# Starting TensorE's streamed operands 64 bytes into their buffers

## The chip, the cores and the metric

The kernel runs on one core of a Trainium2 chip. The metric is device time in microseconds (us) for one execution. Three executions of the kernel before took 458.63, 458.64 and 460.37 us; their median is 458.64 us.

A core has a matrix engine (TensorE, PE in the profile), which multiplies a *stationary* operand that it has loaded ("holds") by a *moving* operand that it streams past it, both read from the on-chip memory SBUF. The load of the stationary operand is an instruction of its own, shown in the profile as the row PEld. VectorE (DVE), ScalarE (ACT) and GpSimd (POOL) do the elementwise work, and DMA queues move data.

## The reference, cut to what matters

The input x has 2048 tokens of 448 channels. Two blocks follow one another, each behind a layer norm whose scale and shift come from a conditioning vector:

```
h = layernorm(x) * (1 + ca) + sa
q, k, v = split(h @ wqkv)                       # 16 heads of 28 channels
pq, pk = phi(q), phi(k)                         # phi(t) = (t > 0 ? t + 1 : exp(t)) + 1e-6
kv = sum over tokens of pk^T v ; z = sum over tokens of pk
x = x + ga * ((pq @ kv) / (pq . z + 1e-6)) @ wo
h = layernorm(x) * (1 + cb) + sb
u = gelu(h^T @ w1 + b1)                         # contraction over the 2048 tokens, 1792 outputs
x = x + gb * (u @ w2 + b2)^T                    # back to the 2048 tokens
```

The data are float32 and the result has to hold that accuracy. The kernel therefore cuts most operands into a high part, rounded to the fast matmul format (float32r), and a low part, the remainder, and forms high*high + high*low + low*high: three fast matmuls for one product.

## The kernel before, in words

**Tiles.** The 2048 tokens are 16 tiles (`t`) of 128 partitions by 448 channels. Nearly every buffer is a slot of one of two pools: `slot` (76 buffers) and, in the first half, `tslot` (25 buffers). Each slot is padded to 512 floats, which is 2048 bytes in every partition, whatever its use. In the allocation of the built program both pools begin 128 bytes past a multiple of 512; an unused constant tile of 96 floats (`space`, line 85) lies ahead of the second pool. A 128-column slice of a slot begins at a multiple of 512 bytes inside it. So a streamed operand, which is a whole slot from its start, and the slice that TensorE holds for it, begin at the same byte address modulo 256 (and modulo 512).

**Stages and their matmuls.** Each matmul listed here streams 448 columns of float32r past 128 held columns, and each needs a load of its own.

- k and q (`project`, line 312): the transposed, normalized tokens (`hh`, `hl`) are held; the weights (`Whi`, `Wlo`, tiles `wh`, `wl`) are streamed. There are 11 matmuls for each of k and q and each token tile but the first, whose products go through plain float32 (`project0`).
- the sums over tokens (`a_outer`, line 394): the tokens (`xh`, `xl`) are held, phi(k) (`pkh`, `pkl`) is streamed; 11 matmuls for each of 16 tiles, accumulated in four PSUM banks `cacc`.
- the output projection (`b_out`, line 654): the transposed scaled phi(q) (`pth`, `ptl`) is held, the folded matrix (`Wph`, `Wpl`) is streamed; 12 matmuls for each of 16 tiles.
- the first product over tokens (`step`, `acc3`, lines 705 to 707): blocks of w1 (`ph`, `pl`) are held, the normalized tokens (`H2h`, `H2l`) are streamed; 3 matmuls for each of 14 output blocks and 16 token tiles.
- the second product over tokens runs in two forms: `mult7` (lines 889 and 890, tiles `ut` and `uw` streamed, one matmul of 448 and one of 224 columns in turn) and `mult1` (again `acc3`, tile `uw` streamed as two runs of 224 columns; the moving operand of line 706 there begins 896 bytes further on than that of 705).

**Order.** The instruction order is written out by hand in one program (`manual_schedule`); engines meet through semaphores only. TensorE's queue therefore has one order through the whole kernel, and the loops over `t` interleave k, the sums, part of q, the projection and the first product so that the other engines' splitting, norms and copies are done ahead of use.

**Who writes the streamed operands.** High parts: ScalarE copies (`w_high` line 176, `a_pk_parts` line 372, `split` line 70, `b_norm2` line 699). Low parts: VectorE subtractions (lines 71, 182, 351, 702), or, for eleven tiles of phi(k) and two of the weights, a ScalarE copy with the sign turned followed by an accumulating DMA from POOL's queue (lines 194 to 195 and 353 to 354).

Of the kernel before, what the change touches and what calls it, by code (L numbers as in the profile page):

```python
# [9 lines left out]
F32R = mybir.dt.float32r  # L10
# [4 lines left out]
P = 128  # L15
S, D, F = 2048, 448, 1792
NT = S // P
NF = F // P
G = 112
# [23 lines left out]
def block_kernel(ctx: ExitStack, tc: tile.TileContext, x, wqkv, wo, w1, b1, w2, b2, c, wmod, out):  # L43
# [16 lines left out]
    def slot(name, w=D, dt=F32, parts=P):  # L60
        return slots.tile([parts, w], dt, name=name, tag="slot", padded_shape=[P, 512])

    def tslot(name, dt=F32, parts=P, w=D):
        return tok.tile([parts, w], dt, name=name, tag="tok", padded_shape=[P, 512])

    def bank(name):
        return psum.tile([P, 512], F32, name=name, tag="bank")

    def split(full, hi, lo):
        nc.scalar.activation(hi, full, AF.Copy)  # L70
        nc.vector.tensor_sub(lo, full, hi.bitcast(F32))  # L71
# [100 lines left out]
    Whi, Wlo = {}, {}  # L172

    def w_high(j, ch):
        Whi[j, ch] = tslot(f"wh{j}_{ch}", F32R)
        nc.scalar.activation(Whi[j, ch], raw_w[j, ch], AF.Copy)

    def w_low(j, ch):
        w, r = Whi[j, ch], raw_w[j, ch]
        if ch < 3:  # L180
            Wlo[j, ch] = tslot(f"wl{j}_{ch}", F32R)
            nc.vector.tensor_sub(Wlo[j, ch], r, w.bitcast(F32))
        else:
            nc.vector.tensor_sub(w[64:128], r[64:128], w[64:128].bitcast(F32))

    def w_low_dma(j, ch):
        w, r = Whi[j, ch], raw_w[j, ch]
        if ch < 3:
            Wlo[j, ch] = tslot(f"wl{j}_{ch}", F32R)
            lo, hi = Wlo[j, ch], w  # L190
        else:
            lo = hi = w[64:128]
            r = r[64:128]
        nc.scalar.activation(lo, hi.bitcast(F32), AF.Copy, scale=-1.0)
        nc.gpsimd.dma_start(lo, r, accum_op=ALU.add)
# [4 lines left out]
    raws, parts = {}, {}  # L200
# [148 lines left out]
    def low(t, lo, full, hi):  # L349
        if t in DVE_LOW:  # L350
            nc.vector.tensor_sub(lo, full, hi.bitcast(F32))
        else:
            nc.scalar.activation(lo, hi.bitcast(F32), AF.Copy, scale=-1.0)
            nc.gpsimd.dma_start(lo, full, accum_op=ALU.add)
# [13 lines left out]

    def a_pk_parts(t):
        pk = pkf.pop(t)  # L370
        hi, lo = slot(f"pkh{t}", dt=F32R), slot(f"pkl{t}", dt=F32R)
        nc.scalar.activation(hi, pk, AF.Copy)
        low(t, lo, pk, hi)
        if t in (0, 1, NT - 1):
            pksum.append(pk)
        elif t == NT - 2:
            pksum14.append(pk)
        else:
            nc.gpsimd.dma_start(pksum[t % 2], pk, accum_op=ALU.add)
        pks[t] = (hi, lo)  # L380
# [62 lines left out]
    a_first((2, 3))  # L443
    keep_warm(2)
    w_high(1, 0)
    a_copy((0, 1))
    a_copy((2,))
    a_copy((3,))
    del tps[0]
    st.pop(0)  # L450
    a_norm_a(1)
    w_high(1, 1)
    a_norm_b(1, sap[:, :D])
    a_dup(1)
    w_low(1, 0)
    w_high(1, 2)
    w_low(1, 1)
    kp0 = project0(1, "kp", lambda: a_transpose(1))
    a_split(1)
    w_high(1, 3)  # L460
    w_low(1, 2)
    w_low(1, 3)
    mod_out(0, sap)
# [3 lines left out]
    for ch in range(4):  # L467
        w_high(0, ch)
    a_exp(0, kp0)
    w_low_dma(0, 0)  # L470
    a_norm_b(2)
    w_low_dma(0, 1)
    a_stats(3)
    a_dup(2)
# [20 lines left out]
    a_exp(2, kp2)  # L495
    a_norm_b(4)
    a_pk_parts(0)
    a_dup(4)
    a_pk(2, kp2)
    a_phi_q()  # L500
    a_pk_parts(1)
    a_q(2)
    a_high(2)
# [6 lines left out]
    for t in range(3, NT):  # L510
# [15 lines left out]
        a_pk(t, kp)  # L526
        a_phi_q()
        a_pk_parts(t - 1)
        if t + 3 < NT:
            a_stats(t + 3)  # L530
# [14 lines left out]
        if t == 4:  # L545
            for g in range(4):
                w = tslot(f"wo{g}", parts=G)
# [58 lines left out]
    H2h, H2l = [None] * NT, [None] * NT  # L606
# [85 lines left out]
    def b_norm2(t, i):  # L692
        rs = rss[i - 1][:, 1:2]
        nb = small.tile([P, 1], F32, name=f"nb{t}", tag="nb")
        nc.gpsimd.tensor_mul(nb, nm2s.pop(t), rs)
        nc.scalar.activation(ys[t], ys[t], AF.Identity, bias=nb, scale=rs)
        H2h[t] = slot(f"h2h{t}", dt=F32R)
        H2l[t] = slot(f"h2l{t}", dt=F32R)
        nc.scalar.activation(H2h[t], ys[t], AF.Copy)

    def b_low2(t):
# [15 lines left out]
    for g in range(4):  # L717
        wp = bank(f"wp{g}")
        nc.tensor.matmul(wp[:G, :D], kvm[:, g * G:(g + 1) * G], wo_sb[g], start=True, stop=True)
        hi = tslot(f"wph{g}", F32R, G)  # L720
        lo = tslot(f"wpl{g}", F32R, G)
        split(wp[:G, :D], hi, lo)
        Wph.append(hi)
        Wpl.append(lo)
# [3 lines left out]
    for i in range(NT + LAG):  # L728
# [11 lines left out]
        t = i - LAG  # L740
# [19 lines left out]
        if norm2:  # L760
            b_norm2(i - 4, i)
# [229 lines left out]
    for o0, n in W1G[1:]:  # L991
# [5 lines left out]
        for r in range(first, NT):  # L997
# [4 lines left out]
            if xleft and k % 2:  # L1002
                t = xleft.pop(0)
# [13 lines left out]
    for n, (kind, p) in enumerate(order):  # L1017
        if jobs:
            jobs.pop(0)()
        while xleft:  # L1020
            t = xleft.pop(0)
# [40 lines left out]
```

## Time and profile before

| what | value |
|---|---|
| median of 3 executions | 458.64 us |
| the profiled execution, its own time | 458.67 us |
| its span in the trace | 457.0 us |
| TensorE matmul busy | 451.6 us, 99% |
| weight loads busy | 409.9 us, 90% |
| VectorE / ScalarE / GpSimd busy | 356.7 / 241.4 / 90.9 us |
| granted TensorE clock | 1.00 |

The busy time of a matmul row counts from its start to a modelled end, and neighbouring matmuls overlap in it: a matmul shown as 365 ns long can be followed by the next one after 203 ns. What a matmul costs in a packed stream is therefore the distance from its start to the next start, here called the *spacing*; it is read from a timeline of starts, or from a stretch that holds nothing else, divided by the count.

### The profile page before, as it was taken

Reading aid. Unit: us, or ns where it says so; the run is one execution under the profiler, and the core shown is the slowest. Engines: PE = TensorE matmul, PEld = TensorE weight load, DVE = VectorE, ACT = ScalarE, POOL = GpSimd, SP = SyncE. Lnnn points to the kernel's source line nnn. Section 1 sums busy time; section 2 is a strip of 40 time slices with the busy share of each in tenths; the row PEclk is TensorE's granted clock in tenths of the full one; section 3 lists DMA queues with packets and bytes.
Section 4 is the critical chain, followed back from the end, with each engine's and each line's share of the span. In section 5 each row is a group of like instructions: output and inputs, shape, how many; then the busy total and the mean of one; then the engine's idle time right before and its main releaser. Section 6 shows DMA issues by size and latency. Waiting matters only on the chain.

```text
span 457.0 us, 7265 instructions
## 1 busy us (share of the span) xinstructions
PE 451.6 (99%) x2378; PEld 409.9 (90%) x2378; DVE 356.7 (78%) x781; ACT 241.4 (53%) x538; POOL 90.9 (20%) x163
## 2 busy tenths in 40 slices
PE   8999999999999999999999999999999999999996
PEld 7689998998799999988999999999999999999996
DVE  5798897878898898896559676629696977798982
ACT  1648766635456576676665445226556262536350
POOL 2215675620014355554300000000000000000000
PEclk9999999999999999999999999999999999999999
DMA  8969999993200003222407453317960583628312
GB/s 228 287 174 174 172 193 227 210 226 116 70 1 2 23 24 103 61 47 48 126 17 230 162 193 106 112 39 227 288 187 23 177 239 113 176 99 250 112 55 98
DMA packets 60550, 61.85 MB, mean 135 GB/s; under 512 B 9248, under 2 KB 53856, under 8 KB 60512
## 3 DMA queue, kind: packets, MB, share of 16 engines
q1 hardware_dynamic: 54752, 52.45, 38.2%
q0 software_dynamic: 5760, 8.95, 12.0%
q8 instruction: 18, 0.29, 0.3%
q14 instruction: 20, 0.16, 0.1%
HBM read 45.09 MB, written 7.34 MB: 115 GB/s over the span
## 4 chain that ended last, share of the span: by engine, by line
PE 90%; ACT 3%; POOL 2%; DVE 1%; DMA 1%; issue 1%; SPq 1%; DVEq 0%
PE y L889 11%; PE up L705 9%; PE up L707 9%; PE up L706 9%; PE cacc L394 8%; PE kp L312 7%; PE qp L312 7%; PE y L890 5%; PE op L654 5%; PE yp L705 4%; PE yp L707 4%; PE yp L706 4%; PE tp L291 1%; DMA wm<-in_w_mod_dram 1%; PE tq L638 1%; PE modp L169 1%
## 5 line engine op out<-in xcount | busy, mean ns | idle before, releaser
L705 PE MATMUL up<-h2h,ph 128*128 128x448 f32 x224 | 82.2, 367 | 0.0
L706 PE MATMUL up<-h2l,ph 128*128 128x448 f32 x224 | 81.8, 365 | 0.0
L707 PE MATMUL up<-h2h,pl 128*128 128x448 f32 x224 | 81.8, 365 | 0.0
L71 DVE TENSOR_TENSOR pl<-pr,ph 128x512 fp32r<-128x512 f32 (+1 forms) x60 | 36.3, 615 | 13.0 <-ACT ph L70 8.3
L706 PEld LDWEIGHTS up<-h2l,ph 128*128 128x128 f32 x224 | 42.1, 188 | 3.5 <-issue 0.2
L705 PEld LDWEIGHTS up<-h2h,ph 128*128 128x128 f32 x224 | 42.1, 188 | 3.5 <-issue 0.2
L707 PEld LDWEIGHTS up<-h2h,pl 128*128 128x128 f32 x224 | 42.1, 188 | 3.4
L70 ACT ACTIVATE ph<-pr 128x512 fp32r<-128x512 f32 (+1 forms) x60 | 32.8, 567 | 16.3 <-PE up L706 11.4
L895 ACT ACTIVATE cc<-y 128x448 f32<-128x448 f32 x15 | 8.2, 545 | 56.5 <-PE y L890 39.8
L705 PE MATMUL yp<-uw,qw 128*128 128x448 f32 x84 | 31.1, 370 | 0.0
L707 PE MATMUL yp<-uw,qw 128*128 128x448 f32 x84 | 30.7, 366 | 0.0
L706 PE MATMUL yp<-uw,qw 128*128 128x448 f32 x84 | 30.7, 365 | 0.0
L394 PE MATMUL cacc<-pkh,xh 128*128 128x448 f32 x64 | 24.8, 387 | 0.0
L654 PE MATMUL op<-wph,pth 112*128 112x448 f32 x64 | 24.7, 386 | 0.0
L654 PE MATMUL op<-wpl,pth 112*128 112x448 f32 x64 | 23.4, 366 | 0.0
L394 PE MATMUL cacc<-pkl,xh 128*128 128x448 f32 x64 | 23.4, 366 | 0.0
L654 PE MATMUL op<-wph,ptl 112*128 112x448 f32 x64 | 23.4, 365 | 0.0
L70 ACT ACTIVATE qw<-q 128x256 fp32r<-128x256 f32 (+1 forms) x56 | 18.9, 352 | 7.7 <-DMA q<-in_B_w_dram 7.0
L312 PE MATMUL kp<-wh,hh 128*128 128x448 f32 x60 | 22.2, 375 | 0.0
L312 PE MATMUL qp<-wh,hh 128*128 128x448 f32 x60 | 22.2, 375 | 0.0
L810 DVE TENSOR_TENSOR u<-u,mod 128x448 f32<-128x448 f32 x14 | 8.7, 620 | 17.1 <-ACT u L809 17.1
L642 ACT ACTIVATE pth<-tq 112x512 fp32r<-112x512 f32 x16 | 9.6, 599 | 23.4 <-PE tq L638 20.4
(198 smaller groups left out, 1242.0 us busy)
## 6 DMA issues: line engine op xcount, KB each, us to landing
pr<-in_B_w_dram SPq DMA_DIRECT2D x48, 256.0 KB, 2.9
a<-in_B_w_dram SPq DMA_DIRECT2D x20, 256.0 KB, 5.2
wm<-in_w_mod_dram SPq DMA_DIRECT2D x24, 196.0 KB, 4.6
a<-in_B_w_dram SPq DMA_DIRECT2D x20, 192.0 KB, 4.9
x<-in_A_x_dram SPq DMA_DIRECT2D x16, 224.0 KB, 4.5
xpark<-x SPq DMA_DIRECT2D x16, 224.0 KB, 1.9
q<-in_B_w_dram SPq DMA_DIRECT2D x28, 128.0 KB, 3.2
xb<-xpark SPq DMA_DIRECT2D x16, 224.0 KB, 4.3
```

Of the source, the lines that this page charges most:

```text
L70: nc.scalar.activation(hi, full, AF.Copy)
L71: nc.vector.tensor_sub(lo, full, hi.bitcast(F32))
L312: nc.tensor.matmul(o, a[:, ch * P:(ch + 1) * P], b, start=(n == 0), stop=(n == 10))
L394: nc.tensor.matmul(cacc[ch][:, :D], a[:, s], b, start=(t == 0 and i == 0), stop=(t == NT - 1 and i == len(todo) - 1))
L642: nc.scalar.activation(phs[t][0], tps[t][:G, :], AF.Copy)
L654: nc.tensor.matmul(opb[t][:, :D], a[:, s], b, start=(n == 0), stop=(n == 11))
L705: nc.tensor.matmul(ps[:, :D], hi[:, sl], mh, start=first, stop=False)
L706: nc.tensor.matmul(ps[:, :D], hi[:, sl], ml, start=False, stop=False)
L707: nc.tensor.matmul(ps[:, :D], lo[:, sl], mh, start=False, stop=last)
L810: nc.vector.tensor_mul(u, u, mods[5])
L889: nc.tensor.matmul(ps[:, :D], h[:, s], w, start=opens and r == 0, stop=False, skip_group_check=True)
L890: nc.tensor.matmul(ps[:, :HD], l[:, s], w[:, :HD], start=False, stop=closes and r == PAIRS - 1, skip_group_check=True)
```

## The change

A helper `moving` takes a slot of the full 512 floats and returns the 448 floats that begin at float 16, so 64 bytes in. The tiles that TensorE streams in five places are made with it: the high and low weights of k and q (`Whi`, `Wlo`), phi(k) (`pkh`, `pkl`), the normalized tokens of the first product (`H2h`, `H2l`) and the folded projection matrix (`Wph`, `Wpl`). What TensorE holds stays where it was. In the built program each of those matmuls now streams from 192 modulo 256 and holds from 128 modulo 256; before, both were at 128. Number, size, order and engine of all instructions stay the same, and so do the number and size of the buffers. Not moved are the operands of the second product (`uw`, `ut`), those of the transposes, and those of the plain float32 matmuls.

```diff
+    def moving(new, name, dt=F32R, parts=P):
+        return new(name, dt=dt, parts=parts, w=512)[:, 16:16 + D]
...
     def w_high(j, ch):
-        Whi[j, ch] = tslot(f"wh{j}_{ch}", F32R)
+        Whi[j, ch] = moving(tslot, f"wh{j}_{ch}")
...
     def w_low(j, ch):
...
-            Wlo[j, ch] = tslot(f"wl{j}_{ch}", F32R)
+            Wlo[j, ch] = moving(tslot, f"wl{j}_{ch}")
...
     def w_low_dma(j, ch):
...
-            Wlo[j, ch] = tslot(f"wl{j}_{ch}", F32R)
+            Wlo[j, ch] = moving(tslot, f"wl{j}_{ch}")
...
     def a_pk_parts(t):
-        hi, lo = slot(f"pkh{t}", dt=F32R), slot(f"pkl{t}", dt=F32R)
+        hi, lo = moving(slot, f"pkh{t}"), moving(slot, f"pkl{t}")
...
-        H2h[t] = slot(f"h2h{t}", dt=F32R)
-        H2l[t] = slot(f"h2l{t}", dt=F32R)
+        H2h[t] = moving(slot, f"h2h{t}")
+        H2l[t] = moving(slot, f"h2l{t}")
...
-        hi = tslot(f"wph{g}", F32R, G)
-        lo = tslot(f"wpl{g}", F32R, G)
+        hi, lo = moving(tslot, f"wph{g}", parts=G), moving(tslot, f"wpl{g}", parts=G)
```

## The prediction

> **What bounds the kernel now.** I read the page's busy shares first, then TensorE's waits, then the stretches by stage, and last single starts, since the change alters no instruction but only where one of TensorE's two reads begins.
>
> ```profile
> span 457.0 us, 7265 instructions
> PE 451.6 (99%) x2378; PEld 409.9 (90%) x2378; DVE 356.7 (78%) x781; ACT 241.4 (53%) x538; POOL 90.9 (20%) x163
> ...
> PE 90%; ACT 3%; POOL 2%; DVE 1%; DMA 1%; issue 1%; SPq 1%; DVEq 0%
> ```
>
> ```profile
> PE warm L133 <- DVE mhalf L87: 1.1, 1, 1.1
> PE tp L411 <- DVE h L406: 0.2, 1, 0.2
> ```
>
> The first fence is the page: the chain that ended last is 90% TensorE. The second is the whole list of TensorE's waits: 1.3 us in 457. So the time is the sum of TensorE's spacings, and whatever changes a spacing by one nanosecond changes the total by the number of such matmuls, as long as the other engines follow. The stretches say how much room they have (columns: stretch, its length, then busy time of PE, PEld, DVE, ACT, POOL with instruction counts, granted clock, DMA share, GB/s):
>
> ```profile
> 30.00:48.00 18.00, 18.00 (x93) 16.48 (x92) 15.07 (x35) 12.31 (x28) 7.29 (x9) 1.00 0.98 207
> 48.00:105.00 57.00, 57.00 (x298) 51.89 (x297) 46.96 (x105) 34.44 (x73) 31.36 (x37) 1.00 0.96 203
> 105.00:135.00 30.00, 30.00 (x157) 25.19 (x156) 26.62 (x49) 16.02 (x32) 1.37 (x4) 1.00 0.18 59
> 135.00:226.00 91.00, 90.75 (x468) 82.84 (x468) 74.88 (x172) 59.69 (x130) 42.58 (x95) 1.00 0.20 53
> 226.00:336.00 110.00, 110.00 (x546) 101.95 (x546) 74.88 (x163) 53.74 (x120) 1.02 (x4) 1.00 0.49 154
> 336.00:400.00 64.00, 64.00 (x375) 60.29 (x375) 50.61 (x106) 29.53 (x69) 0.00 (x0) 1.00 0.50 146
> ```
>
> The clock is full throughout, so no spacing can be blamed on it. VectorE is 68 to 89% busy in the stretches that the change touches (up to 336 us): it would follow a TensorE some per cent faster. The tightest resource is DMA between 30 and 105 us, 0.96 to 0.98.
>
> **What one matmul costs.** The next two fences are timelines of TensorE and of its weight loads (start, length, line, tiles).
>
> ```profile
> 249.93 0.36 PE L707 MATMUL up<-h2h,pl 128*128 128x448 f32 x1
> 250.13 0.36 PE L705 MATMUL up<-h2h,ph 128*128 128x448 f32 x1
> 250.34 0.36 PE L706 MATMUL up<-h2l,ph 128*128 128x448 f32 x1
> ...
> 254.19 0.36 PE L707 MATMUL up<-h2h,pl 128*128 128x448 f32 x1
> ```
>
> ```profile
> 250.14 0.19 PEld L706 LDWEIGHTS up<-h2l,ph 128*128 128x128 f32 x1
> 250.34 0.19 PEld L707 LDWEIGHTS up<-h2h,pl 128*128 128x128 f32 x1
> ```
>
> From 249.93 to 254.19 there are 21 spacings, so 202.9 ns each. Over the whole first product the same follows from one stretch, with the `up` tiles alone (99.08 us for 489 matmuls, 202.6 ns):
>
> ```profile
> 226.00:336.00 110.00, 99.08 (x489) 91.46 (x488) 8.72 (x14) 1.00 0.49 154
> ```
>
> The load of the next stationary operand starts 0.01 us after each matmul's start, so the two reads always set off together, and before the change from the same address modulo 256. Is anything lost by that? The plain float32 matmuls of line 719 stream 448 columns too, at a slower pace:
>
> ```profile
> 120.28 3.17 PE L719 MATMUL wp<-wo,kvm 112*112 112x448 f32 x8
> ...
> L719 PE MATMUL wp<-wo,kvm 112*112 112x448 f32 x8 | 3.2, 538 | 0.0
> ```
>
> Seven spacings and a last length of 0.538 make 3.17, so one is 376 ns. If the fast format streams at just twice that pace (an estimate, which no row shows alone), it needs 188 ns, and some 15 ns of the 202.7 are lost in the fast format only. That the loss depends on how the two reads meet is hinted at by a second value which the same instructions take for stretches at a time:
>
> ```profile
> 34.95 0.37 PE L394 MATMUL cacc<-pkh,xh 128*128 128x448 f32 x1
> ...
> 40.74 0.37 PE L312 MATMUL kp<-wh,hh 128*128 128x448 f32 x1
> ```
>
> These are 28 spacings in 5.79 us: 206.8 ns each, 4 ns more than elsewhere at the same sizes, addresses modulo 256 and clock. Something as small as the phase between the two streams moves the spacing by 4 ns.
>
> **The change part by part.** It adds and removes no instruction. How many matmuls stream from the new place follows from the code, checked by one row of each group:
>
> ```profile
> L705 PE MATMUL up<-h2h,ph 128*128 128x448 f32 x224 | 82.2, 367 | 0.0
> L394 PE MATMUL cacc<-pkl,xh 128*128 128x448 f32 x64 | 23.4, 366 | 0.0
> L654 PE MATMUL op<-wph,ptl 112*128 112x448 f32 x64 | 23.4, 365 | 0.0
> L312 PE MATMUL kp<-wh,hh 128*128 128x448 f32 x60 | 22.2, 375 | 0.0
> ```
>
> First product 3 x 224 = 672, sums 16 x 11 = 176, projection 3 x 64 = 192, k and q 2 x 15 x 11 = 330: 1370 matmuls, about 278 us at 203 ns. One nanosecond of spacing is 1.37 us.
>
> *The price of the shift* is not in the trace: no row streams from 64 bytes beside what is loaded. From below it is bounded by the loss itself, 15 ns for each, 20.5 us in all (438 us). From above the nearest rows are the spacing in the slower phase, +4 ns or +5.5 us (464.2), and, further off, the 448-column matmuls of line 889, which begin less than 110 ns after their own load and so meet two loads instead of one:
>
> ```profile
> 401.19 0.38 PE L889 MATMUL y<-uw,s4h 128*128 128x448 f32 x1
> 401.40 0.26 PE L890 MATMUL y<-uw,s4l 128*128 128x224 f32 x1
> ```
>
> That is 0.21 us, +7 ns, or 9.6 us over 1370 (468.3). The nearest of these rows is the step of 4 ns, because it is seen on the very instructions that move. I take it as the size, and downwards as the sign. Upwards would mean that at the old place the streams already meet little; but 15 ns of loss on each matmul say that they meet often, and equal start addresses, with both reads set off within 10 ns, are the case in which two readers of one memory begin in the same part of it. Sum: 1370 x 4 ns = 5.5 us less. The profiled execution took 458.67 us, 457.0 of span and 1.7 around it, and stands 0.03 over the median of 458.64: 453.2 us.
>
> *The writers of the moved tiles* write 64 bytes further on, with the same counts and sizes. I cost that at nothing: TensorE waits for none of them now. Were it dearer, the cover is the distance of a writer from its reader. The thinnest is that of the low parts finished by DMA:
>
> ```profile
> pkl<-pk POOLq DMA_DIRECT2D x11, 224.0 KB, 3.8
> ...
> wl<-wr POOLq DMA_DIRECT2D x2, 224.0 KB, 6.1
> ```
>
> ```profile
> 41.49 0.86 POOL L354 DMA_DIRECT2D pkl<-pk  x1 [3.06 <-ACT h L283]
> ```
>
> ```profile
> 48.92 0.37 PE L394 MATMUL cacc<-pkl,xh 128*128 128x448 f32 x1
> ```
>
> The first `pkl` by DMA is issued at 41.49 and lands some 3.8 us later, at 45.3; the sums that read it begin to do so at 48.92, so a landing may be late by 3.6 us before TensorE stands. If it doubled (7.6 us), TensorE would wait 0.2 us at most at each of eleven tiles, 2.2 us. Queued behind it on POOL are the other adding DMAs and the small steps of the norms. A gain brings the reader closer: between two groups of sums lie 33 or so matmuls, 0.13 us at 4 ns each, which this margin holds too.
>
> **The rule of the Trainium skill that speaks against any effect.** The rows above show load and stream side by side and a spacing of 202.6 ns. The Trainium skill, "TensorE: Matmul & The Clock Gate", section "Part 2: What happens when you issue a matmul", says that TensorE reads SBUF through two independent ports and that loading the next weights takes nothing from the running matmul; by it the starting addresses cannot matter and the time stays 458.7. Its formula for matmuls issued back to back, N/2.4 + 2.5 ns, would give 189 ns for 448 columns; the trace has 202.6, so something of 13 ns is not in the rule, and the rule's claim is weakened but not disproved.
>
> **Rivals.**
>
> *No change.* The loss of 15 ns could belong to the fast format or to the swap of weights and not to addresses. For it speaks the second product, where each third matmul (line 706) streams from 128 bytes beside what is loaded, and the others from the same place:
>
> ```profile
> 450.29 0.36 PE L706 MATMUL yp<-uw,qw 128*128 128x448 f32 x1
> ...
> 452.73 0.36 PE L706 MATMUL yp<-uw,qw 128*128 128x448 f32 x1
> ```
>
> Twelve spacings in 2.44 us, 203.3 ns: nothing gained by 128 bytes. Against it speak the two phases. If two reads side by side came around every 128 bytes, 64 would be the opposite phase and 128 no evidence. Time: 458.7 us.
>
> *Slower.* The two streams run at different paces (a load of 128 columns takes most of a spacing, a matmul streams 448 in it), so they meet several times in any case, and 64 bytes only move where. If the old start had put the streams just past one another, the new one adds a meeting to each matmul: 206.8 ns throughout is 1370 x 4 = +5.5 us, 464.2; two steps are +11 us, 469.7. It decides as soon as the moved groups stand above 204.4 ns (0.5%, 2.3 us, over 1370). For it speaks that the trace already shows 206.8 for whole groups of equal addresses, so a worse phase exists and is stable.
>
> *Most of the loss goes.* If 64 bytes part the streams for good, the spacing nears 189 to 193 ns, and the time 440 to 445 us. Then DMA between 30 and 105 us becomes the question: some 330 of the 391 matmuls in these two stretches are moved ones, and their 10 to 14 ns would shorten them by 3 to 5 us of 75, with DMA at 0.96 to 0.98 now; two thirds of that part of the gain could turn into waits for data, some 3 us.
>
> **How the numbers follow.** About 0.5% (2.3 us) is what a measurement can tell from no change. Chances: a step of about 4 ns faster 0.32 (449 to 456 us), most of the loss gone 0.18 (440 to 449), no change 0.12, slower by about a step 0.25 (462 to 467), slower by more 0.13 (467 to 472). Faster is 0.50, same 0.12, slower 0.38. The likeliest single case is the step faster, 453.2 us. The range from 442 to 467 leaves out the lowest part of the second case (0.05) and the last case (0.13).
>
> **What would show it.** In the changed kernel's trace, right: starts of the `up` matmuls 199 ns apart instead of 203, the stretch of `up` alone shorter by 2% (489 matmuls in about 97 us instead of 99), the same drop in `cacc`, `op`, `kp` and `qp`, and in the second product, which isn't moved, 203 and 0.31 us for a pair of lines 889 and 890 as now. TensorE's list of waits would stay near 1.3 us; if it grows between 30 and 105 us with DMA as releaser, the third rival's limit is met. Wrong: moved groups at 202 to 204 (no change) or 207 and more (slower), with weight loads still starting 0.01 us after the matmul, would say that the sign of the address term, which I could only argue, failed; a changed second product would say that something else than the address differs between the programs.

## The result, and the profile after

The changed kernel takes 456.79 us (median of 10 executions, 455.70 to 458.10) against 459.07 us (10 executions, 458.63 to 461.26): a ratio of 0.9945 with a 95% interval of 0.9927 to 0.9962, so 2.3 us or half a per cent faster. Sent again later it gave 456.59 against 458.95 us, 0.9954 (0.9939 to 0.9969). The forecast was 453.2 us: the direction held, and the gain is less than half of the 5.5 us.

The profiled execution took 457.18 us, with a span of 455.5. These are lines of its page; the first two answer to the first fence of the prediction.

```profile
span 455.5 us, 7265 instructions
PE 448.9 (99%) x2378; PEld 410.5 (90%) x2378; DVE 356.8 (78%) x781; ACT 241.5 (53%) x538; POOL 91.3 (20%) x163
...
PE 84%; ACT 4%; DVE 4%; POOL 3%; DMA 3%; issue 1%; SPq 0%; POOLq 0%; DVEq 0%
```

TensorE's share of the chain that ended last fell from 90 to 84%, and VectorE, DMA and the others have what it lost. Next, TensorE's starts in the first product, which answer to the prediction's timeline:

```profile
250.04 0.36 PE L711 MATMUL up<-h2h,pl 128*128 128x448 f32 x1
250.24 0.36 PE L709 MATMUL up<-h2h,ph 128*128 128x448 f32 x1
250.44 0.36 PE L710 MATMUL up<-h2l,ph 128*128 128x448 f32 x1
250.64 0.36 PE L711 MATMUL up<-h2h,pl 128*128 128x448 f32 x1
```

Three matmuls now take 0.60 us, where they took 0.61. To see small differences of spacing I use one stretch in which every kernel runs nothing but the first product and count its matmuls: the `up` tiles from 230 to 320 us (columns: stretch, length, busy time and count of PE, of PEld, of ACT, clock, DMA share, GB/s). In the kernel before, then after:

```profile
230.00:320.00 90.00, 90.00 (x446) 83.40 (x445) 7.47 (x12) 1.00 0.43 137
```

```profile
230.00:320.00 90.00, 90.00 (x451) 84.36 (x451) 7.46 (x12) 1.00 0.45 140
```

Two of each count reach over the edges. From the starts themselves the mean spacing in this stretch is 202.7 ns before and 200.0 ns after. Over all moved groups (the spacings up to 225 ns, so without those that hold a wait) it is 203.21 and 200.37 ns: 2.84 ns less, and 1370 x 2.84 ns = 3.9 us. The slower phase of 206 to 207 ns is gone: among runs of nine moved matmuls, 10% had a mean of 205.5 ns or more before, and none has after. (Single spacings don't show this: in the faster phase of before, too, one matmul in five takes 206 or 207 ns.) The second product, which isn't moved, is the same to 0.1 ns.

So some 3.9 us were saved on the spacing and 2.3 arrived. The list of TensorE's waits has two new lines:

```profile
PE warm L137 <- DVE mhalf L91: 1.1, 1, 1.1
PE cacc L398 <- DMA pkl<-pk: 0.8, 1, 0.8
PE tq L642 <- DVE pn L631: 0.6, 2, 0.4
PE tp L415 <- DVE h L410: 0.2, 1, 0.2
```

### The profile page after: what moved, and what is told of

Same layout as the page of the kernel before. It is cut to its first block, busy times and chain, and to the rows that moved or that the text cites. A ratio compares the mean times of both kernels' runs of the same rounds, so it can differ in the third digit from the quotient of the medians.

```text
span 455.5 us, 7265 instructions
## 1 busy us (share of the span) xinstructions
PE 448.9 (99%) x2378; PEld 410.5 (90%) x2378; DVE 356.8 (78%) x781; ACT 241.5 (53%) x538; POOL 91.3 (20%) x163
## 4 chain that ended last, share of the span: by engine, by line
PE 84%; ACT 4%; DVE 4%; POOL 3%; DMA 3%; issue 1%; SPq 0%; POOLq 0%; DVEq 0%
PE y L892 11%; PE up L711 8%; PE up L710 8%; PE up L709 8%; PE qp L316 7%; PE cacc L398 6%; PE y L893 5%; PE kp L316 5%; PE yp L709 4%; PE yp L711 4%; PE yp L710 4%; PE op L658 4%; PE warm L137 2%; DMA pkl<-pk 2%; PE modp L173 1%
## 5 line engine op out<-in xcount | busy, mean ns | idle before, releaser
L709 PE MATMUL up<-h2h,ph 128*128 128x448 f32 x224 | 81.1, 362 | 0.0
L75 DVE TENSOR_TENSOR qw<-q,qw 128x256 fp32r<-128x256 f32 (+1 forms) x56 | 18.9, 352 | 3.9 <-ACT qw L74 3.9
L316 PE MATMUL kp<-wh,hl 128*128 128x448 f32 x60 | 21.7, 367 | 0.1
```

The lines of the kernel that those rows point to most:

```text
L316: nc.tensor.matmul(o, a[:, ch * P:(ch + 1) * P], b, start=(n == 0), stop=(n == 10))
L709: nc.tensor.matmul(ps[:, :D], hi[:, sl], mh, start=first, stop=False)
```

## The experiments

Theory A, at the start: the loss of some 15 ns on each matmul arises where the stream meets the load beside it, and the distance of their starting addresses modulo 256 sets how often. Its rivals: the place of the stream alone counts (C); the loss belongs to the fast format, and addresses only shift a phase (F). For the missing gain: waits into which a faster TensorE always runs (L), or the accident of one execution (M).

**Is it the distance modulo 256?** Three kernels begin the moved tiles elsewhere; a fourth is the kernel before with everything moved alike.

```diff
-        return new(name, dt=dt, parts=parts, w=512)[:, 16:16 + D]
+        return new(name, dt=dt, parts=parts, w=512)[:, 64:64 + D]
```

Float 64 is 256 bytes; the other two kernels have 32 (128 bytes) and 48 (192 bytes) in its place.

> The moved tiles begin 256 bytes into their slots instead of 64, so that stream and held operand are again equal modulo 256 but not equal in address within the slot. If the relation modulo 256 sets the spacing (theory A), the first product goes back to 202.6 ns, stretches at 206 to 207 ns come back, and the time is that of before within 0.3%. If it is enough that the stream begins anywhere but at its slot's start (theory B), the spacing stays at 200 ns and the time near 0.994 of before. If the period is longer than 256 bytes, a third value shows.

> The moved tiles begin 128 bytes in. If streams that start in opposite halves of a 256-byte period meet least (theory A1), the spacing falls below the 200 ns of 64 bytes, to 197 or less, and the time to 0.990 or less. If the period is 128 bytes (theory A2), the spacing is 202.6 ns and the time that of before. The second product of before, where one matmul in three streams 128 bytes off at an unchanged 203 ns, speaks for A2.

> The moved tiles begin 192 bytes in, which is 64 bytes short of equal modulo 256. If the period is 128 bytes, this is the same as 64 bytes: 200 ns and 0.994 to 0.995 of before. If the period is 256 bytes and the order of the two streams matters (stream ahead against stream behind), the spacing differs from that of 64 bytes by 1 ns or more in the first product.

```diff
+    pad = ctx.enter_context(tc.tile_pool(name="pad", bufs=1))
+    pad.tile([P, 16], F32, name="pad")
     slots = ctx.enter_context(tc.tile_pool(name="slots", bufs=NSLOT))
```

> The kernel before with every buffer 64 bytes further on, by an unused tile ahead of all pools: stream and held operand both begin at 192 modulo 256. If the distance between the two counts (theory A), spacing and time are those of before: 202.6 ns, with stretches at 206 to 207 ns, ratio 1.000 within 0.003. If the place of the stream alone counts (theory C), 200 ns and 0.994 or, with the second product shifted too, less.

Two more starts, 32 and 96 bytes (floats 8 and 24), were run later, to see the form of the curve:

> The moved tiles begin 32 bytes in. So far the mean spacing of the moved groups is 203.2, 200.4, 204.2 and 202.3 ns at 0, 64, 128 and 192 bytes and 203.0 again at 256. If this is one smooth wave over 256 bytes (theory S), 32 bytes give 201 to 202.5 ns and 0.996 to 0.999. If the memory has parts of 64 bytes and only the part counts (theory P), 32 bytes are much like 0 or like 64. If 64 is a lucky value among irregular ones, 32 may be anything from 199 to 207.

> The moved tiles begin 96 bytes in. Theory S: between 200.4 and 204.2 ns, some 202 ns and 0.998. Theory P: like 64 or like 128 bytes. A value below 200 ns, and with it a ratio under 0.994, would be a kernel that beats both.

The results together; the spacing is the mean over all moved groups, as above, and the last column is the mean in the first product's undisturbed part (from 218 us on). The ratio is of several executions, but both spacings are read from one profile of each kernel:

| stream begins, bytes past the held operand's start modulo 256 | ratio to before, 95% interval | spacing, ns | first product, ns |
|---|---|---|---|
| 0 (before) | 1 | 203.2 | 202.7 |
| 32 | 1.0064 (1.0045 to 1.0083) | 205.6 | 206.7 |
| 64 (the change) | 0.9945 (0.9927 to 0.9962) | 200.4 | 200.0 |
| 96 | 1.0053 (1.0035 to 1.0070) | 205.3 | 205.3 |
| 128 | 1.0024 (1.0014 to 1.0034) | 204.2 | 204.0 |
| 192 | 0.9996 (0.9985 to 1.0007) | 202.3 | 202.2 |
| 256 | 1.0002 (0.9985 to 1.0020) | 203.0 | 202.7 |
| 0, both moved by 64 | 1.0003 (0.9988 to 1.0017) | 203.1 | 202.7 |

The counts in the same stretch, for both moved by 64, for 128 and for 32 bytes, in this order:

```profile
230.00:320.00 90.00, 90.00 (x446) 83.40 (x445) 7.48 (x12) 1.00 0.42 135
```

```profile
230.00:320.00 90.00, 90.00 (x443) 82.84 (x443) 7.48 (x12) 1.00 0.42 134
```

```profile
230.00:320.00 90.00, 90.00 (x437) 81.98 (x436) 7.49 (x12) 1.00 0.40 131
```

The distance counts, and 256 bytes bring the old value back: C falls, since a stream at 192 modulo 256 is fast only where the held operand is at 128. 128 bytes are not like 0, so the period isn't 128. The curve is no smooth wave: 32 and 96 bytes are the worst, with 64 the best between them. Of the starts tried only 64 gains.

**Do waits eat the rest, and where?** The change once more, then each half of it, then the second product added.

> The changed kernel once more, unaltered, as the measure for the next three and as a second profile. The first profile gave 200.4 ns as the mean spacing of the moved groups against 203.2 before, 1370 x 2.84 ns = 3.9 us, while the median fell by 2.3 us. If the missing 1.6 us are waits that a faster TensorE runs into in every execution (theory L), this profile shows the spacing again and again more than 1 us of waits between 70 and 210 us, for DMA or VectorE. If they were the accident of one execution (theory M), the waits are gone here and the ratio of the medians is nearer to 0.9915.

The spacing came out as before, 200.4 ns, and the ratio 0.9954. TensorE's waits:

```profile
PE warm L137 <- DVE mhalf L91: 1.1, 1, 1.1
PE tq L642 <- DVE pn L631: 0.6, 2, 0.3
PE kp L316 <- DVE hl L75: 0.2, 1, 0.2
PE tp L415 <- DVE h L410: 0.2, 1, 0.2
```

The wait for the adding DMA has left the list, and the waits for VectorE are there again (L). What waits cost, listed or not, is seen in the stretch from the fourth k product to the last projection, the same work in both kernels, before and then the run just told (busy times of PE, PEld, DVE, ACT, POOL):

```profile
31.63:212.28 180.65, 180.40 (x938) 162.50 (x936) 155.96 (x339) 114.52 (x244) 76.29 (x130) 1.00 0.49 110
```

```profile
32.25:211.65 179.40, 178.61 (x937) 162.26 (x936) 155.85 (x339) 114.64 (x244) 76.55 (x130) 1.00 0.49 108
```

It became 1.25 us shorter. 774 moved matmuls start in it; the mean spacing of those that hold no wait fell from 203.55 to 200.72 ns, which makes 2.2 us: 0.9 us were given back here. Both kernels issue the same matmuls in the same order, so the distances between starts can be compared one by one. Six of them grew by more than 25 ns, and these make 0.87 us: 0.24 and 0.10 at two transposes of the scaled phi(q) (`tq`), 0.24 and 0.10 at two k products, and 0.08 and 0.11 at the first reader of one `pkl` finished by DMA and just behind it. So the DMA still cost something here, below what the list shows: only the size of this wait is an accident of the execution (M). In the first profile of the change the same sum is 1.75 us, 1.09 of it at that DMA.

The waits for the scaled phi(q) are not new. These lines are of the kernel before and then of this run:

```profile
195.53 0.36 PE L707 MATMUL up<-h2h,pl 128*128 128x448 f32 x1
196.01 0.62 PE L638 MATMUL tq<-ident,pn 128*112 128x128 f32 x4
```

```profile
194.72 0.37 PE L711 MATMUL up<-h2h,pl 128*128 128x448 f32 x1
195.44 0.62 PE L642 MATMUL tq<-ident,pn 128*112 128x128 f32 x4 [0.34 <-DVE pn L631]
```

Most `tq` groups start 0.20 to 0.21 us after the matmul ahead of them. This one starts 0.47 us after it in the kernel before and 0.71 in the change (by the unrounded starts); another, at 206.94 us of before, starts 0.50 us after it, and 0.60 in the change. So TensorE already stood for 0.27 and 0.29 us there. The list of waits is silent about it, since it counts from the modelled end of the matmul ahead (0.36 us after its start) and does not list the 0.11 and 0.14 us that are left. The chain that ended last does show it. In the kernel before it leaves TensorE behind one `tq` group and comes back to it 32 us later:

```profile
174.60 0.45 PE tq L638 x4
...
206.26 0.54 DVE pn L627
...
206.94 0.62 PE tq L638 x4
```

Between these it runs through ScalarE, GpSimd and VectorE alone. There a faster TensorE only waits longer.

In the packed rest of the first product nothing was given back. Its same 529 matmuls, before and in this run:

```profile
217.91:324.92 107.01, 107.01 (x529) 98.97 (x527) 7.88 (x13) 1.00 0.46 143
```

```profile
217.22:322.83 105.61, 105.61 (x529) 98.86 (x527) 7.85 (x13) 1.00 0.46 145
```

1.40 us less, and 529 x 2.67 ns are 1.41. So 3.9 us of spacing less 0.9 us of waits are 3.0 us for this profile, and 3.9 less 1.75 are 2.1 us for the first one. The interval of the first measurement (0.9927 is 3.4 us, 0.9962 is 1.7 us) holds both; 3.0 lies above that of the second. The beginning, before any moved matmul has run, differs by some 1 us from profile to profile (the first modulation product starts at 7.8 to 9.0 us, by the landing of its weights), so the sum cannot be closed more finely.

> Only k, q, the sums and the projection stream from 64 bytes on; the first product streams from its slots' starts as before. 698 matmuls at 3.15 ns less (203.6 to 200.4) are 2.2 us, 0.9952, if nothing else waits. By theory L most of the lost time is in this part, so that 0.997 or 0.998 is left, with waits in the profile for the adding DMA of phi(k) or for the scaled phi(q).

```diff
-        H2h[t] = moving(slot, f"h2h{t}")
-        H2l[t] = moving(slot, f"h2l{t}")
+        H2h[t] = slot(f"h2h{t}", dt=F32R)
+        H2l[t] = slot(f"h2l{t}", dt=F32R)
```

This was slower than before, 460.26 us, ratio 1.0024 (1.0012 to 1.0036). The early stages did gain, as the count of their starts shows (200 to 201 ns in every moved group, and 1.1 us won between 31.6 and 212 us). The loss is in the first product, whose operands stand exactly where they stood before:

```profile
230.00:320.00 90.00, 90.00 (x437) 81.76 (x436) 7.47 (x12) 1.00 0.43 135
```

437 instead of 446: the whole stretch ran in the slower phase, 206.7 ns on the mean, and lost 529 x 4 ns = 2.1 us. Nothing in it differs from the kernel before but the moment at which it began. At equal starts a packed stretch was thus seen in two phases, and as far as this one profile shows, what runs ahead of it settles which one it takes.

> Only the first product streams from 64 bytes on. 672 matmuls at 2.5 ns less (202.8 to 200.25) are 1.7 us, ratio 0.9963. From 226 us on no other engine is near its limit, so by theory L this part keeps nearly the whole of it (0.996 to 0.997); about a fifth of its matmuls lie among the projection's, where it may be lost. Early stages as before, without a wait for the adding DMA.

```diff
-        H2h[t] = slot(f"h2h{t}", dt=F32R)
-        H2l[t] = slot(f"h2l{t}", dt=F32R)
+        H2h[t] = moving(slot, f"h2h{t}")
+        H2l[t] = moving(slot, f"h2l{t}")
```

457.40 us, 0.9967 (0.9954 to 0.9980), as expected: 200.0 ns in the undisturbed part, no new wait in TensorE's list. This half alone carries two thirds of the change's gain.

> The changed kernel with the streamed operands of the second product 64 bytes on as well (an unused tile of 16 floats ahead of one pool, and the helper for the other tiles). If the address term acts in it as in the first, its 252 matmuls of lines 705 to 707 lose 2 to 3 ns, 0.6 us, and its 245 pairs of 448 and 224 columns 3 to 5 ns, 1 us: 0.996 to 0.997 of the changed kernel. If the pairs are set by the weight loads, which follow one another after 108 ns there, they stay at 313 ns. The matmul of line 706 there then streams at 192 beside its next load, which at 192 bytes everywhere gave 202.3 ns on the mean.

```diff
-        w = slot(f"u{name}_{r}", dt=F32R)
+        w = moving(slot, f"u{name}_{r}")
...
+    uparts.tile([P, 16], F32, name="upad")
     HD = D // 2
```

456.40 us, 0.9953 (0.9935 to 0.9972), the same as the change alone. The 448-column matmuls of the pairs went from 211.4 to 210.8 ns, those of 224 from 101.6 to 103.1, so a pair became 0.9 ns longer, and the 252 others went from 204.5 to 203.8 ns: plus 0.2 and minus 0.2 us.

The last run on this question gives two blocks of w1 to VectorE, because the chain of waits in the projection's stretch runs through ScalarE and POOL, which cut these blocks:

```diff
-PIECE_DMA = range(14, 18)
+PIECE_DMA = range(14, 16)
```

> The changed kernel with blocks 16 and 17 of w1 cut by VectorE (0.62 us each) instead of by a second ScalarE copy (0.65 us) and an adding DMA issued by POOL (0.97 us). If the waits of TensorE for the scaled phi(q) at tiles 13 and 15 (0.6 us) are bound by that ScalarE and POOL chain, they go and the time falls by up to 0.6 us, ratio to before 0.993 to 0.995. If VectorE itself is the limit there, as its 86% busy suggests, the waits grow by up to 0.6 us each and the ratio is 0.996 or more.

456.32 us, 0.9949 (0.9931 to 0.9967); one wait for the scaled phi(q), 0.4 us, is left of two. The first `tq` group still starts 0.74 us after the matmul ahead of it, the second 0.46 instead of 0.60. That the chain took part in the second is likely, but the time cannot be told from that of the change alone, so this stays undecided.

**Does the load beside the stream make the loss at all?** Now it is tested whether the 15 ns shrink with the load. The kernels of this part leave out some of the work. Their times are single executions (457.68, 459.01, 459.17, 459.49 and 440.61 us in the order told here, against 458.7 to 459.0 for the kernel before), so they are read by their spacing, from one profile each. In the first run one matmul of three in the first product holds 64 of its 128 columns; in its control only the order differs.

```diff
-            acc3(ps, hi, lo, slice(i * P, (i + 1) * P), mh, ml, first, last)
+            nc.tensor.matmul(ps[:, :D], hi[:, sl], mh, start=first, stop=False)
+            nc.tensor.matmul(ps[:64, :D], lo[:, i * P:i * P + 64], mh, start=False, stop=False)
+            nc.tensor.matmul(ps[:, :D], hi[:, sl], ml, start=False, stop=last)
```

> The kernel before; in the first product the second and third matmul of each three change places, and the one with the low part of w1 holds only the first 64 of its 128 columns. Left out: the low part of w1 for the other 64 outputs of each block. Its load, which runs beside the matmul ahead of it (high times high), reads half as much. If the 15 ns that are lost on each matmul are lost to the load beside it (theory A), that matmul's spacing falls by about half of them, from 202.7 to 195 or 196 ns, and the two others stay. If they belong to the fast format or to the swap (the rival that address and load play no part), all three stay at 202.7 ns.

> The control for the run with half a load: the same change of places of two matmuls in the first product, with all 128 columns held. The three spacings should be 202.6 ns on the mean, or 206 to 207 ns if the stretch falls into the slower phase, as it did in the run that moved only k, q, the sums and the projection.

The control had 202.7 ns. With half a load the matmul beside it took 206.6 ns, more and not less, and its neighbours 200.9 and 199.2: 202.2 on the mean. The next two runs shorten two loads of three to 32 columns, at the old and at the new starts.

```diff
+            a, b = i * P, i * P + 32
+            todo = [(ps[:32, :D], lo[:, a:b], mh), (ps[:32, :D], hi[:, a:b], ml)]
+            todo.insert(2 if last else 0, (ps[:, :D], hi[:, a:a + P], mh))
```

> The kernel before; in the first product two of each three matmuls (those with a low part) hold only 32 of 128 columns. Left out: the low parts' share for 96 of 128 outputs of each block. If the 15 ns belong to the reading of the load beside the stream (theory A), the two matmuls that run beside a short load take 188 to 193 ns and the third 203. If the loss is the fast format's own or that of the swap of weights (theory F), all three stay between 199 and 203 ns on the mean.

> The same on the changed kernel, whose streams begin 64 bytes on. Against the run with short loads at the old starts: theory A, no difference beside the short loads, since little is left to be met; theory F with an address term from the start of each load, 2 to 3 ns less again, as with whole loads.

Weight loads of the first of them, then the stretch's count for it and for the second:

```profile
249.95 0.19 PEld L716 LDWEIGHTS up<-h2h,ph 128*128 128x128 f32 x1
250.16 0.11 PEld L716 LDWEIGHTS up<-h2h,pl 128*32 128x32 f32 x1
250.35 0.11 PEld L716 LDWEIGHTS up<-h2l,ph 128*32 128x32 f32 x1
```

```profile
230.00:320.00 90.00, 90.00 (x447) 59.86 (x446) 7.46 (x12) 1.00 0.42 136
```

```profile
230.00:320.00 90.00, 90.00 (x442) 59.21 (x441) 7.47 (x12) 1.00 0.43 135
```

The loads' busy time fell from 83.4 to 59.9 us, and the mean spacing hardly moved: 202.3 ns. Single ones did move: the two matmuls beside a short load took 197.7 and 205.8 ns, the one beside a whole load 203.4. Theory A in its strong form falls, since it asked for 188 to 193 beside a short load: the loss is not made by the volume that the load reads. And with short loads the start at 64 bytes was slower (204.4 ns) than the old one, so 64 does not look like a good distance in itself; but each of these values is from one profile, and a stretch can have two phases.

The last run also halves what the two matmuls with short loads stream:

```diff
-            todo = [(ps[:32, :D], lo[:, a:b], mh), (ps[:32, :D], hi[:, a:b], ml)]
+            todo = [(ps[:32, :224], lo[:, a:b], mh[:, :224]), (ps[:32, :224], hi[:, a:b], ml[:, :224])]
```

> The kernel with short loads at the old starts; the two matmuls of each three that hold 32 columns also stream only 224 of 448. Left out besides: the low parts' share for the other 224 channels. The matmul with 224 columns that runs beside a load of 32 columns is the one to read. If the loss is a fixed price of a matmul (some 14 ns), its spacing is 94 + 14 = 108 ns; if it goes with the columns, 101 ns; if neither, 94 to 96 ns.

```profile
250.28 0.27 PE L716 MATMUL up<-h2h,pl 128*32 128x224 f32 x1
250.39 0.27 PE L716 MATMUL up<-h2l,ph 128*32 128x224 f32 x1
250.49 0.38 PE L716 MATMUL up<-h2h,ph 128*128 128x448 f32 x1
...
250.70 0.27 PE L716 MATMUL up<-h2h,pl 128*32 128x224 f32 x1
250.81 0.27 PE L716 MATMUL up<-h2l,ph 128*32 128x224 f32 x1
```

VectorE can't keep up with this kernel, so the means hold waits; most spacings beside a short load are 101 to 105 ns, and their median is 104. That lies between a price that goes with the columns (101) and a fixed one (108), so this run does not tell the two apart. What 448 columns would take without a load beside them no run shows.

## Why the prediction was right or wrong

- *What bounds the kernel.* Right in the main: the moved spacings were the only thing that changed on TensorE's own account, and where they grew the time followed (at 32 bytes +2.4 ns, by 1370 matmuls 3.3 us, and 0.64% or 2.9 us measured; at 128 bytes +1.0 ns, 1.4 and 1.1 us). Where they shrank it followed in part only: at 192 bytes -0.9 ns would be 1.2 us, and 0.2 were measured (at most 0.7 by the interval).
- *The sign.* The text argued that equal starts are the case in which the two reads meet most. The direction came out as said, the argument did not hold: 32, 96 and 128 bytes are slower than equal starts, and 192 bytes save 0.9 ns without a gain in time that could be told. It was one start of the five tried off the old one, not any parting of the streams; that the change had this one was luck.
- *The size: the failed step.* "I take the step of 4 ns" was mis-sized: the moved groups gained 2.84 ns, 3.9 us in place of 5.5. The 4 ns were the distance between two phases at one address, and I carried them over to a change of address. The change in fact does two things: the faster phase goes from 202.7 to 200.0, and the slower one no longer occurs in any profile with whole loads and all the moved operands at 64 bytes.
- *The cover by the other engines: the second failed step.* "So the time is the sum of TensorE's spacings" rested on a list of waits of 1.3 us and on a chain that is 90% TensorE. Neither was read far enough: the other 10% hold the 32 us up to 206.94 us in which ScalarE, GpSimd and VectorE set the time, and the list is silent about the 0.27 and 0.29 us for which TensorE already stood there. "It would follow a TensorE some per cent faster", said of VectorE at 68 to 89% busy, was therefore wrong: between 31 and 212 us, 0.9 of 2.2 us was given back in one profile and 1.75 in the other. The faster TensorE is, the longer it stands at those two transposes: they start 0.32 to 0.41 us after the matmul ahead of them at 32, 96 and 128 bytes, 0.47 to 0.50 in the kernel before and at 256, 0.52 to 0.56 at 192, and 0.54 to 0.74 in the four profiles at 64 whose blocks are cut as before.
- *The adding DMA.* I gave it a margin of 3.6 us and a cost of nothing. That margin was read at the first of eleven transfers. The thinnest is at the sixth, here in the kernel before:

```profile
66.21 0.86 POOL L354 DMA_DIRECT2D pkl<-pk  x1 [0.82 <-ACT pkl L353]
```

```profile
73.50 0.37 PE L394 MATMUL cacc<-pkl,xh 128*128 128x448 f32 x1
```

This transfer landed 7.1 us after its issue, at 73.35, and so 0.14 us before its first reader started. In five of the six profiles with phi(k) at 64 bytes that reader started 0.04 us after the landing, and 0.08 to 0.99 us later than at its usual pace; two of these waits, of 0.7 and 0.8 us of idle time, are in the lists. The landing took 6.6 to 8.1 us with phi(k) at 64 bytes and 5.8 to 7.4 elsewhere; whether the change itself lengthens it is not shown. The row of landing times shows the tail that the median, on which I counted, hides. First before, then after:

```profile
DMA to landing us min/median/max: 3.1/3.8/7.1
```

```profile
DMA to landing us min/median/max: 3.1/3.9/8.1
```

- *The bound of 15 ns from below.* That the fast format needs 188 ns was an estimate, and no run bears it out: no packed stretch of 448-column matmuls had a mean under 200.0 ns, whatever the start, nor under 202.2 with shorter loads. At most 2.7 of the 15 ns were won, so no run shows the room that I gave to the third rival (440 to 445 us). Whether the rest is the format's pace or a price of each matmul stays open.
- *The rule of the Trainium skill* ("TensorE: Matmul & The Clock Gate", section "Part 2: What happens when you issue a matmul"), that a load takes nothing from the running matmul, holds here on the mean for the load's length: 128 or 32 columns, 202.7 or 202.3 ns. The distance of the two starting addresses, which has no part in the rule, moves the spacing between 200 and 207 ns.
- *The rivals.* No change and slower were priced from the right rows: 206.7 ns is what 32 bytes cost, and what the first product took when only the other stages were moved.

What exactly meets at these addresses stays open. That the term depends on the distance of stream and held operand modulo 256 is shown for whole loads. That its sign turns when two loads of three are short rests on one profile each. A mechanism that gives 200.0 ns at 64 bytes and 206.7 at 32 is not shown.

## What to carry to other kernels

Where a packed stream of matmuls sets the time, the start of the streamed operand against the held one is worth a scan in steps of 32 bytes over 256, measured by the count of matmuls in a fixed stretch: here it is worth from -0.6% to +0.6%, and no rule but the measurement told which. Compare such variants by the spacing and by the whole time, since the phase of a later stretch can turn a local gain into a loss (the run with k, q, the sums and the projection alone). And before a gain on the bounding engine is counted in full, follow the chain through the stretches where it leaves that engine, and compare the distances between starts at each matmul that depends on another engine or on a transfer: the list of waits was silent about 0.29 us here, and two to four fifths of that stretch's gain stayed there.

## What the runs showed of the hardware that was not expected

- The same matmuls at the same addresses run at 202.7 or at 206.7 ns for a hundred microseconds on end, as it seems by what ran ahead of them (206.7 at equal starts in one profile, 202.7 in four); at 64 bytes distance, with whole loads, only 200.0 ns was seen in that stretch, in five profiles of four kernels.
- At 128 bytes the starts follow each other in a cycle of five, 196, 203, 212, 200 and 209 ns, though all three kinds of matmul in it have the same sizes; at equal starts, in the faster phase, it is a cycle of five too, 199, 207, 202, 203 and 202 ns, and at 64 bytes one of three, 197, 202 and 201 ns.
- Holding 32 columns instead of 128 in two matmuls of three shortens their loads from 0.19 to 0.11 us and the mean spacing by 0.4 ns only.
